# Attention and two gated layers: the score products of a head grouped by their number of rows

## The chip, the core and the metric

The kernel runs on one core of one Trainium2 chip. The metric is the device time of one execution in microseconds (us). TensorE (PE, with its weight loads listed apart as PEld), VectorE (DVE), ScalarE (ACT), GpSimd (POOL) and the DMA queues run beside each other and wait for each other by semaphores.

## The reference

The shapes are batch 2, 12 heads, 448 tokens, 64 dimensions a head; the model width is 768, the hidden width 1536. The operands of the three gated products arrive as float64 words, which the kernel decodes itself.

```python
scores = matmul(q, k^T) / sqrt(64)            # per batch and head: 448 x 448
scores = cap * tanh(scores / cap)
attn   = exp(scores - max) ; attn /= sum(attn)
x      = matmul(attn, v)                      # all heads side by side: 896 x 768
x      = (silu(x @ w_gate) * (x @ w_val)) @ w_out          # 768 -> 1536 -> 768
out    = (sigmoid(x @ w2_gate) * (x @ w2_val)) @ w2_out
```

## The kernel before

Precision is kept with float32r parts: a value is split into a high and a low part, and a product is the sum of high times high, low times high and high times low. In the attention, a head has only 64 dimensions, so the first two of the three terms are stacked into one product over 128 rows: the stationary operand `kk` holds k_high in 64 rows and k_low in the other 64, and the moving operand `qq` holds q_high twice. The third term, k_high times q_low (`kh`, `qlo`), has 64 rows.

The 24 heads are handled one after another, two to a pair. Within a head the keys are cut into four blocks of 112 (`CP`), and each block gives one 112 x 448 score tile in a PSUM bank of its own. `scores(n)` makes them in two halves. A half takes a two-bank tile `pss` from a pool of two such tiles (`bank2`), so the two halves of a head use the two buffers and the next head uses the same two again. For each of its two blocks, PE makes the 128-row product (line 410, which starts the sum) and then the 64-row product (line 411, which ends it). ACT then takes the tanh of the half (line 412) and, after both halves, the exponential of the whole head (line 416).

The order of work on every engine is written by hand in the loop over heads n. PE gets, in an even head: the 8 score products, 8 transposes for the pair after next (line 348), and the products of head n-2 with V (`values`, line 454). An odd head has the same without the transposes. In the values products a part of the blocks is computed in whole float32 and the rest in float32r parts (`eh`, `el`, `vh`, `vl`), all with 112 rows. Heads 0 to 3 are special: the first values products come ahead of head 2's scores, and there are none at all between heads 0 and 1 and between heads 2 and 3. DVE makes the parts and the normalisation (lines 352 to 356, 426, 428, 393, 397, 483, 468, 486), ACT copies each values result out (`xu`, line 457), POOL issues six small copies by DMA for each pair and makes `xl` (line 488). SP issues the loads and the DMAs of the denominators.

From head 21 on, DVE and ACT also decode the first weight blocks (lines 74 to 84). After the last head, PE alternates the first gated products (`products`, line 154) with the values of the last two heads; the last pair's `x` reaches them through line 488. Then follow the two gated layers.

Of the kernel before, what the change touches and what calls it, by code (L numbers as in the profile page):

```python
# [19 lines left out]
def attention_then_two_gated_layers(  # L20
# [14 lines left out]
    nc = tc.nc  # L35
    B, H, S, D = q.shape
# [3 lines left out]
    R = 4  # L40
    CP = S // R
# [4 lines left out]
    WIDEST = 32.0  # L46
# [5 lines left out]
    def bank2(name):  # L52
        return ps.tile([P, 2, 512], F32, tag="p2", name=name, bufs=2)
# [10 lines left out]
    wp = ctx.enter_context(tc.tile_pool(name="wp", bufs=2))  # L64

    def decode(r, hi, lo):
        """float64 words to hi + lo, each of which a float32r holds exactly or rounds last."""
        n = r.shape[1] * r.shape[2]
        w2 = r.rearrange("p k f -> p (k f)").bitcast(U32).rearrange("p (n two) -> p n two", two=2)
        low, top = w2[:, :, 0], w2[:, :, 1]  # L70
        t = wp.tile([P, n], U32, tag="t", name="t", bufs=1)
        c = wp.tile([P, n], U32, tag="c", name="c", bufs=2)
        g = wp.tile([P, n], F32, tag="g", name="g", bufs=1)
        nc.vector.tensor_scalar(t, top, 0x7FFFFFFF, 9, ALU.bitwise_and, ALU.logical_shift_right)  # L74
        nc.scalar.activation(c, t, AF.Relu, bias=bias_sb, scale=4096.0)  # L75
        yield
        nc.vector.tensor_scalar(g.bitcast(U32), top, 0x1FF, None, ALU.bitwise_and)
        nc.vector.scalar_tensor_tensor(g, low, 2.0**-32, g.bitcast(U32), ALU.mult, ALU.add)  # L78
        yield
        nc.vector.scalar_tensor_tensor(c, top, 0x80000000, c, ALU.bitwise_and, ALU.bitwise_or)  # L80
        nc.scalar.copy(hi, c.bitcast(F32).rearrange("p (k f) -> p k f", k=r.shape[1]))  # L81
        yield
        nc.vector.tensor_scalar(t, c, 0xFF800000, None, ALU.bitwise_and)
        nc.vector.scalar_tensor_tensor(  # L84
            lo,
            g.rearrange("p (k f) -> p k f", k=r.shape[1]),
            2.0**-20,
            t.bitcast(F32).rearrange("p (k f) -> p k f", k=r.shape[1]),
            ALU.mult,
            ALU.mult,  # L90
        )

    class Stream:
        """Weight blocks in the order of their use, loaded and decoded ahead of it."""

        def __init__(self, jobs):
            self.keys = list(jobs)
# [50 lines left out]
        return [bank1("pv0")[:, :S], bank1("pv1")[:, :S]]  # L148

    def products(o, w, bh, bl, u, ks, nk, off=0):  # L150
        """Adds the blocks ks of w^T x for half u of the tokens to o, in float32r parts."""
        for kk in ks:
            for m, (a, x) in enumerate(((w[0], bh), (w[0], bl), (w[1], bh))):
                nc.tensor.matmul(  # L154
                    o,
                    lhsT=a[:, kk - off, :],
                    rhs=x[:, kk, halves[u]],
                    start=(kk == 0 and m == 0),
                    stop=(kk == nk - 1 and m == 2),
                )  # L160

    # The weight blocks in the order they are decoded: 128 columns at a time, a layer's gate and
    # value in turn. The last product takes its weights as moving operand, in two wide blocks of
    # columns; the first of them is decoded during the second layer's gate and value.
    ZB = (320, 448)
    ZW = 64
    early = [(0, 4), (0, 9), (2, 2), (2, 4), (1, 5)]
# [34 lines left out]
            z_job(1, c)  # L202
        return Stream(jobs), pools, z_tiles

# [1 line left out]
    def hidden(ws, hp, sp, layer, func, bh, bl, begun):  # L206
        hh = hp.tile([P, KF, NT], F32R, tag="hh", name="hh")
        hl = hp.tile([P, KF, NT], F32R, tag="hl", name="hl")
# [76 lines left out]
                        m += rows  # L285
                e0 += ne

# [1 line left out]
    pairs = [(b, p) for b in range(B) for p in range(NP)]  # L289
    NPAIR = len(pairs)  # L290
    NHEAD = 2 * NPAIR
# [1 line left out]
    with ExitStack() as actx:  # L293
        ap = actx.enter_context(tc.tile_pool(name="ap", bufs=2))
        dr = actx.enter_context(tc.tile_pool(name="dr", bufs=2, space=bass.MemoryType.DRAM))
        fix = actx.enter_context(tc.tile_pool(name="fix", bufs=1))
        # Products of zeros that keep the tensor engine awake until the data comes.
        warm = ap.tile([P, 512], mybir.dt.bfloat16, tag="x", name="warm", bufs=2)
        nc.vector.memset(warm, 0.0)
        pw = bank1("pw")  # L300
# [38 lines left out]
            ]  # L339

        def transposed(i):
            """K and Q of a pair of heads with the head's dimension on partitions, as float32r
            parts, and stacked so that 128 rows carry k_hi q_hi + k_lo q_hi."""
            got = []
            for t in raw[i][:2]:
                pt = bank1("pt")
                for c in range(R):
                    nc.tensor.transpose(pt[:, c * CP : (c + 1) * CP], t[:, c, :, :], ident[:CP, :CP])
                got.append(pt[:, :S])
            pk, pq = got  # L350
            ka, kb, qa, qb, ql, kl = operand_tiles()
            nc.vector.tensor_copy(kb, pk)
            nc.vector.tensor_copy(qa, pq)
            yield
            nc.vector.tensor_tensor(kl, pk, kb.bitcast(F32), ALU.subtract)
            nc.vector.tensor_tensor(ql, pq, qa.bitcast(F32), ALU.subtract)
            nc.gpsimd.dma_start(qb[A], qa[Z])
            nc.gpsimd.dma_start(qb[Z], qa[Z])
            nc.gpsimd.dma_start(ka[A], kb[A])
            nc.gpsimd.dma_start(ka[Z], kl[A])  # L360
            nc.gpsimd.dma_start(kb[A], kl[Z])
            nc.gpsimd.dma_start(qa[Z], qa[A])
            operands[2 * i] = (ka, qa, ka[A], ql[A])
            operands[2 * i + 1] = (kb, qb, kb[Z], ql[Z])
            yield

        def transposed_apart(i, j, tiles, copy):
            """The same for one head of the pair, without the way over a DMA."""
            got = []
            for t in raw[i][:2]:  # L370
                pt = bank1("pt")
                for c in range(R):
                    nc.tensor.transpose(pt[A, c * CP : (c + 1) * CP], t[:, j, c, :], ident[:CP, :CP])
                got.append(pt[A, :S])
            pk, pq = got
            kk, qq, qlo = tiles[j], tiles[2 + j], tiles[4 + j]
            nc.vector.tensor_copy(kk[A], pk)
            copy(qq[A], pq)
            copy(qq[Z], pq)
            nc.vector.tensor_tensor(kk[Z], pk, kk[A].bitcast(F32), ALU.subtract)  # L380
            nc.vector.tensor_tensor(qlo[A], pq, qq[A].bitcast(F32), ALU.subtract)
            operands[2 * i + j] = (kk, qq, kk[A], qlo[A])
# [19 lines left out]
        def scores(n):  # L402
            kk, qq, kh, qlo = operands.pop(n)
            e = ap.tile([CP, R, S], F32, tag="e", name="e", bufs=3)
            for half in range(2):
                h = slice(2 * half, 2 * half + 2)
                pss = bank2("pss")
                for u in range(2):
                    c = slice((2 * half + u) * CP, (2 * half + u + 1) * CP)
                    nc.tensor.matmul(pss[:CP, u, :S], lhsT=kk[:, c], rhs=qq, start=True, stop=False)  # L410
                    nc.tensor.matmul(pss[:CP, u, :S], lhsT=kh[:, c], rhs=qlo, start=False, stop=True)  # L411
                nc.scalar.activation(e[:, h], pss[:CP, :, :S], AF.Tanh, scale=inv_sb[:CP])  # L412
                if n == 0:
                    nc.scalar.activation(e[:, h], e[:, h], AF.Exp, scale=near_sb[:CP])
            if n > 0:
                nc.scalar.activation(e, e, AF.Exp, scale=near_sb[:CP])
            ex[n] = e
# [17 lines left out]
        rb = {}  # L435

        def values(n):
            """The head's numerators and, in the row below them, denominators; both from whole
            float32 products or from float32r parts."""
            i, j = divmod(n, 2)  # L440
            e = ex.pop(n)
            tv = raw[i][2]
# [2 lines left out]
            if m:  # L445
                eh, el = eparts.pop(n)
                vh, vl = vparts.pop(n)
                for c in range(m):
                    w = R - m + c
# [42 lines left out]
            for _ in g:  # L492
                pass

        # How many of a head's key blocks go through float32r parts in the product with V, by what
        # the vector engine has time for beside the first weight blocks.
        nsplit = [0, 1, 2, 3] + [2, 3] * 9 + [1, 1]
        load(0, apart=True)
        cap_sb = const.tile([P, 1], F32, name="cap_sb")
# [84 lines left out]
    wide = nc.values_load(wide_sb[0:1, 0:1], min_val=0, max_val=1, skip_runtime_bounds_check_because="the result of a comparison")  # L584
    gated_layers(ws, pools, z_tiles, xh, xl, begun)

# [1 line left out]
    # Up to WIDEST the cap itself keeps exp(score) and the sums far inside of float32's range, and  # L588
    # the sums so far above the guard of 1e-9 (it is relative to the largest term) that it doesn't
    # reach their last place. Beyond, the attention is done over with the maximum of each row taken  # L590
    # off, and the guard.
    with tc.If(wide != 0):
        xh = const.tile([P, KD, NT], F32R, tag="xh", name="xh_any")
        xl = const.tile([P, KD, NT], F32R, tag="xl", name="xl_any")
        with ExitStack() as gctx:
# [9 lines left out]
            for b, p in pairs:  # L605
                kt = gp.tile([P, S], F32, tag="kt", name="kt")
                qt = gp.tile([P, S], F32, tag="qt", name="qt")
                for dst, src in ((kt, k), (qt, q)):
                    t = gp.tile([CP, R, 2, D], F32, tag="t", name="t")
# [5 lines left out]
                for j in range(2):  # L615
                    rows = slice(j * D, (j + 1) * D)
# [3 lines left out]
                    for c in range(R):  # L620
                        pss = bank1("pss")
# [67 lines left out]
```

## Time and profile before

| | |
|---|---|
| time of 3 runs | 690.79, 692.37, 692.53 us |
| median | 692.37 us |
| profiled execution, from its first to its last instruction (span) | 689.1 us |
| PE busy (matmul) | 681.2 us, 99% |
| DVE busy | 490.2 us, 71% |
| ACT busy | 297.1 us, 43% |
| granted TensorE clock, mean | 0.998 of full speed |

For the profiled execution the page gives its span and no time beside it; the median of the runs lies 3.2 us above the span, and the span is taken as the execution's time less these. A busy PE is not PE at its peak, since matmuls are pipelined and their ends are modelled: a row's own duration says little, and what a product costs is read from the distance between its start and the start of the next.

### The profile page before, as it was taken

The page shows a single profiled execution, that of the slowest core. Times are in us where ns is not written, and L with a number is a line of the kernel's source. Part 1 is how long each engine was busy: PE and PEld are TensorE (multiplying, and loading weights), DVE is VectorE, ACT ScalarE, POOL GpSimd, SP SyncE. Part 2 cuts the span into 40 slices and gives each one's busy share as a digit, 9 for nine tenths or more (in the row PEclk, how much of TensorE's full clock was granted, in tenths as well). Part 3 has the DMA queues.
Part 4 walks back from the last instruction along what each step waited for, and adds up shares of the span by engine and source line. Part 5 has one row for each costly group of instructions (what it writes and reads, how often), then busy time and mean ns, then how long its engine had stood idle before and what let it go on. Part 6 is the DMA issues. An engine that isn't in the chain of part 4 may idle for free. (4 is left out here: it accounts for less than half of the span.)

```text
span 689.1 us, 8475 instructions
## 1 busy us (share of the span) xinstructions
PE 681.2 (99%) x3218; PEld 567.0 (82%) x3218; DVE 490.2 (71%) x746; ACT 297.1 (43%) x369; POOL 46.5 (7%) x80
## 2 busy tenths in 40 slices
PE   9999999999999999999999999999999999999996
PEld 5455455458999999999999999999999999999995
DVE  6567877887798977799687976677798676495000
ACT  6767677762543443344343434333344333242000
POOL 1332333210000000000000000000000000000000
PEclk9999999999999999999999999999999999999999
DMA  8565756233224442344433443322344323062011
GB/s 204 104 133 127 191 135 153 53 106 119 93 93 137 138 137 93 92 137 138 136 113 119 142 133 119 111 92 92 103 143 142 117 92 92 26 205 67 27 41 31
DMA packets 107327, 77.98 MB, mean 113 GB/s; under 512 B 35472, under 2 KB 106512, under 8 KB 107280
## 3 DMA queue, kind: packets, MB, share of 16 engines
q1 hardware_dynamic: 102208, 70.28, 33.8%
q0 software_dynamic: 4800, 6.89, 4.7%
q8 instruction: 27, 0.44, 0.3%
q10 hardware_dynamic: 272, 0.20, 0.1%
q14 instruction: 20, 0.16, 0.1%
HBM read 67.63 MB, written 2.80 MB: 102 GB/s over the span
## 5 line engine op out<-in xcount | busy, mean ns | idle before, releaser
L75 ACT ACTIVATE c<-t,bias_sb 128x768 uint32<-128x768 uint32 x72 | 67.6, 940 | 88.4 <-DVE t L74 88.4
L81 ACT CAST wh<-c 128x768 fp32r<-128x768 f32 x60 | 50.3, 838 | 78.1 <-DVE c L80 78.1
L80 DVE SCALAR_TENSOR_TENSOR c<-r,c 128x768 uint32<-128x768 uint32 x72 | 68.5, 952 | 4.3 <-ACT c L75 4.2
L78 DVE SCALAR_TENSOR_TENSOR g<-r,g 128x768 f32<-128x768 uint32 x72 | 69.0, 958 | 2.5
L412 ACT ACTIVATE e<-pss,inv_sb 112x896 f32<-112x896 f32 x48 | 48.3, 1007 | 28.8 <-PE pss L411 22.1
L227 DVE TENSOR_TENSOR sg<-pv,sg 128x448 f32<-128x448 f32 x48 | 29.7, 619 | 43.1 <-PE pv L154 39.8
L84 DVE SCALAR_TENSOR_TENSOR wl<-g,t 128x768 fp32r<-128x768 f32 x60 | 58.3, 972 | 2.1
L228 ACT CAST hh<-sg 128x448 fp32r<-128x448 f32 x48 | 27.2, 567 | 72.3 <-DVE sg L227 71.6
L154 PE MATMUL pg<-xl,wh 128*128 128x448 f32 x144 | 52.8, 367 | 0.0
L154 PE MATMUL pg<-xh,wl 128*128 128x448 f32 x144 | 52.7, 366 | 0.0
L154 PE MATMUL pv<-yl,wh 128*128 128x448 f32 x144 | 52.7, 366 | 0.0
L154 PE MATMUL pv<-yh,wh 128*128 128x448 f32 x144 | 52.7, 366 | 0.0
L154 PE MATMUL pv<-xh,wh 128*128 128x448 f32 x144 | 52.7, 366 | 0.0
L154 PE MATMUL pg<-yh,wl 128*128 128x448 f32 x144 | 52.7, 366 | 0.0
L154 PE MATMUL pg<-yl,wh 128*128 128x448 f32 x144 | 52.7, 366 | 0.0
L154 PE MATMUL pg<-xh,wh 128*128 128x448 f32 x144 | 52.7, 366 | 0.0
L154 PE MATMUL pv<-xh,wl 128*128 128x448 f32 x144 | 52.7, 366 | 0.0
L154 PE MATMUL pg<-yh,wh 128*128 128x448 f32 x144 | 52.7, 366 | 0.0
L154 PE MATMUL pv<-xl,wh 128*128 128x448 f32 x144 | 52.7, 366 | 0.0
L154 PE MATMUL pv<-yh,wl 128*128 128x448 f32 x144 | 52.7, 366 | 0.0
L154 PE MATMUL pg<-hl,wh 128*128 128x448 f32 x144 | 52.6, 365 | 0.0
L154 PE MATMUL pg<-hh,wl 128*128 128x448 f32 x144 | 52.6, 365 | 0.0
(125 smaller groups left out, 1454.5 us busy)
## 6 DMA issues: line engine op xcount, KB each, us to landing
r<-in_moe_w_gate_dram SPq DMA_DIRECT2D x24, 768.0 KB, 4.3
r<-in_moe_w_val_dram SPq DMA_DIRECT2D x24, 768.0 KB, 4.3
r<-in_moe_w_out_dram SPq DMA_DIRECT2D x24, 768.0 KB, 4.2
vt<-in_v_dram SPq DMA_DIRECT2D x24, 112.0 KB, 3.2
rb<-d SPq DMA_DIRECT2D x12, 224.0 KB, 3.3
tk<-in_k_dram SPq DMA_DIRECT2D x10, 224.0 KB, 3.2
tq<-in_q_dram SPq DMA_DIRECT2D x10, 224.0 KB, 3.9
qb<-qa POOLq DMA_DIRECT2D x20, 112.0 KB, 2.3
```

Of the source, the lines that this page charges most:

```text
L75: nc.scalar.activation(c, t, AF.Relu, bias=bias_sb, scale=4096.0)
L78: nc.vector.scalar_tensor_tensor(g, low, 2.0**-32, g.bitcast(U32), ALU.mult, ALU.add)
L80: nc.vector.scalar_tensor_tensor(c, top, 0x80000000, c, ALU.bitwise_and, ALU.bitwise_or)
L81: nc.scalar.copy(hi, c.bitcast(F32).rearrange("p (k f) -> p k f", k=r.shape[1]))
L84: nc.vector.scalar_tensor_tensor(lo, g.rearrange("p (k f) -> p k f", k=r.shape[1]), 2.0**-20, t.bitcast(F32).rearrange("p (k f) -> p k f", ...
L154: nc.tensor.matmul(o, lhsT=a[:, kk - off, :], rhs=x[:, kk, halves[u]], start=(kk == 0 and m == 0), stop=(kk == nk - 1 and m == 2),)
L227: nc.vector.tensor_tensor(sg, vs[u], sg, ALU.mult)
L228: nc.scalar.copy(hh[:, f, halves[u]], sg)
L412: nc.scalar.activation(e[:, h], pss[:CP, :, :S], AF.Tanh, scale=inv_sb[:CP])
```

## The change

The four 128-row products of a head come first, then its four 64-row products. To do so both `pss` tiles are taken at the head's start. The products, their operands, the sum in each bank and the ACT instructions are the same as before. The rest of the diff empties docstrings and comments and leaves the code as it is.

```diff
         e = ap.tile([CP, R, S], F32, tag="e", name="e", bufs=3)
-            for half in range(2):
+            cols = [slice(c * CP, (c + 1) * CP) for c in range(R)]
+            banks = [bank2("pss") for _ in range(2)]
+            for c in range(R):
+                nc.tensor.matmul(banks[c // 2][:CP, c % 2, :S], lhsT=kk[:, cols[c]], rhs=qq, start=True, stop=False)
+            for c in range(R):
+                nc.tensor.matmul(banks[c // 2][:CP, c % 2, :S], lhsT=kh[:, cols[c]], rhs=qlo, start=False, stop=True)
+            for half, pss in enumerate(banks):
                 h = slice(2 * half, 2 * half + 2)
-                pss = bank2("pss")
-                for u in range(2):
-                    c = slice((2 * half + u) * CP, (2 * half + u + 1) * CP)
-                    nc.tensor.matmul(pss[:CP, u, :S], lhsT=kk[:, c], rhs=qq, start=True, stop=False)
-                    nc.tensor.matmul(pss[:CP, u, :S], lhsT=kh[:, c], rhs=qlo, start=False, stop=True)
                 nc.scalar.activation(e[:, h], pss[:CP, :, :S], AF.Tanh, scale=inv_sb[:CP])
```

## Rows read from the trace of the kernel before

**Rows 1.** The page: span, and busy time, share and instructions of the engines.
```profile
span 689.1 us, 8475 instructions
...
PE 681.2 (99%) x3218; PEld 567.0 (82%) x3218; DVE 490.2 (71%) x746; ACT 297.1 (43%) x369; POOL 46.5 (7%) x80
```

**Rows 2.** Busy time in stretches: engines in us (instructions), clock, DMA share, GB/s.
```profile
0.00:147.00 147.00, 145.52 (x531) 74.02 (x532) 110.56 (x199) 104.94 (x101) 45.10 (x79) 1.00 0.58 136
...
165.00:689.00 524.00, 517.75 (x2612) 479.84 (x2610) 365.61 (x525) 185.58 (x261) 0.00 (x0) 1.00 0.34 107
```

**Rows 3.** Timeline of PE, head 15: start us, duration us, line, out<-in, rows*columns.
```profile
95.03 0.57 PE L454 MATMUL pv<-el,vh 112*65 112x448 f32 x2
95.44 0.36 PE L410 MATMUL pss<-qb,kb 128*112 128x448 f32 x1
95.74 0.46 PE L411 MATMUL pss<-ql,kb 64*112 64x448 f32 x1
...
96.51 0.46 PE L411 MATMUL pss<-ql,kb 64*112 64x448 f32 x1
...
98.44 0.97 PE L454 MATMUL pv<-e,vt 112*65 112x448 f32 x2
...
101.07 0.37 PE L410 MATMUL pss<-qa,ka 128*112 128x448 f32 x1
```

**Rows 4.** Timeline of the weight loads of the same head, with idle time before.
```profile
95.24 0.18 PEld L410 LDWEIGHTS pss<-qb,kb 128*112 128x112 f32 x1
95.73 0.17 PEld L411 LDWEIGHTS pss<-ql,kb 64*112 64x112 f32 x1 [0.32 <-issue]
96.12 0.17 PEld L410 LDWEIGHTS pss<-qb,kb 128*112 128x112 f32 x1 [0.22 <-issue]
```

**Rows 5.** Waits of the weight loads, 0 to 165 us: us in total, times, longest.
```profile
PEld pss L411 <- issue: 22.2, 94, 0.3
```

**Rows 6.** Timeline of the engines, the lines of ACT for the scores of head 15.
```profile
97.00 1.01 ACT L412 ACTIVATE e<-pss,inv_sb 112x896 f32<-112x896 f32 x1 [0.83 <-DVE el L428]
...
98.55 1.01 ACT L412 ACTIVATE e<-pss,inv_sb 112x896 f32<-112x896 f32 x1 [0.54 <-PE pss L411]
...
99.59 1.79 ACT L416 ACTIVATE e<-e,near_sb 112x1792 f32<-112x1792 f32 x1
...
101.29 0.52 ACT L457 COPY xu<-pv 65x448 f32<-65x448 f32 x1
```

**Rows 7.** Timeline of PE, starts of heads 1, 2 and 3.
```profile
11.59 0.44 PE L410 MATMUL pss<-qb,kb 128*112 128x448 f32 x1
...
18.10 0.71 PE L410 MATMUL pss<-qa,ka 128*112 128x448 f32 x1
...
22.18 0.43 PE L410 MATMUL pss<-qb,kb 128*112 128x448 f32 x1
```

**Rows 8.** Timeline of ACT, the second tanh of heads 0 and 2.
```profile
10.62 0.99 ACT L412 ACTIVATE e<-pss,inv_sb 112x896 f32<-112x896 f32 x1
...
21.53 1.01 ACT L412 ACTIVATE e<-pss,inv_sb 112x896 f32<-112x896 f32 x1 [0.53 <-PE pss L411]
```

**Rows 9.** Busy time over one pair (heads 16 and 17), columns as in rows 2.
```profile
101.10:113.25 12.15, 12.15 (x47) 6.21 (x45) 9.59 (x17) 8.54 (x9) 4.61 (x7) 1.00 0.79 198
```

**Rows 10.** Timeline of DVE: first work of that pair, and of the next.
```profile
104.72 0.62 DVE L352 CAST kb<-pt 128x448 fp32r<-128x448 f32 x1 [2.52 <-PE pt L348]
...
116.86 0.62 DVE L352 CAST kb<-pt 128x448 fp32r<-128x448 f32 x1 [2.48 <-PE pt L348]
```

**Rows 11.** Busy time in heads 20 to 23, columns as in rows 2.
```profile
125.40:150.00 24.60, 24.60 (x80) 11.52 (x79) 20.36 (x37) 20.09 (x21) 2.54 (x2) 1.00 0.20 61
```

**Rows 12.** Timeline of DVE: the last pair's low part, and a decode step before it.
```profile
159.16 0.96 DVE L80 SCALAR_TENSOR_TENSOR c<-r,c 128x768 uint32<-128x768 uint32 x1 [1.76 <-ACT c L75]
...
170.03 0.63 DVE L488 TENSOR_TENSOR xl<-x,xh 128x448 fp32r<-128x448 f32 x1
```

**Rows 13.** Timeline of PE: the first product with that low part.
```profile
171.51 0.37 PE L154 MATMUL pg<-xl,wh 128*128 128x448 f32 x1
```

## The prediction

> **What bounds the kernel now.** Begin with the page's busy times: PE shows 99% of the span, far above DVE and ACT [rows 1]. A busy PE need not be a well-used one, so the next view is the busy time by stretch: in the attention (0 to 147 us) the weight loads are busy for half of the time, in the gated layers for 92% of it, and PE has next to no idle time in either [rows 2]. The same engine is thus full in both, but something in the attention makes its products longer. The timeline of PE shows what. Products of 112 rows follow each other at 0.205 us: two of them start at 95.03, the next group at 95.44 [rows 3]. The first score product after them has 128 rows and starts without a gap, so 112 and 128 rows go together. From there on 128-row and 64-row products alternate, and seven starts from 95.74 to 98.44 are (98.44 - 95.74) / 7 = 0.386 us apart, although each moves the same 448 columns. The weight loads tell why: the load for the first product is done 0.2 us ahead of it, during the product before, while from then on each load starts only when its own product is listed as starting, after 0.2 to 0.3 us of idle time [rows 4]. Of the 96 loads of 64-row weights, 94 waited so [rows 5]. So every change between 128 and 64 rows costs PE 0.386 - 0.205 = 0.18 us, about half on each side: the first score product, loaded ahead, is followed after 0.30 us (0.09 for the end of the old product), the others after 0.386 (0.09 more for the load in the open).
>
> That the two products of a block add into the same bank isn't the reason: the 112-row products of one head add into one bank too, at 0.205 us.
>
> **The change, part by part.** Removed are six of a head's eight changes of row count. Before: 128 to 64 four times, 64 to 128 or 112 four times (the last into what follows the head). After: one each. The operations are the same in number and shape. No DMA is issued in this step, so no queue is passed; ACT's order (tanh, tanh, exponential) stays.
>
> The saving is 6 x 0.18 = 1.08 us a head. The head in the rows takes 98.44 - 95.44 = 3.00 us for its score products and will take 1.92; 24 heads give 25.9 us, if two things hold.
>
> The first is that 64-row products follow each other as closely as 112- and 128-row products do. No row shows two of them in a row. The bounds are 0.205 us (the nearest rows by kind: float32r, 448 columns, one shape after the same shape) and 0.386 us (the nearest by operands: the same 64-row product among 128-row ones). I take 0.205, since the loads that come late in these rows all follow a product with another number of rows. At the upper bound the three steps from 64 to 64 save nothing and 24 x 3 x 0.18 = 13.0 us are lost; halfway (0.295, where only the load is in the open), 6.5.
>
> The rows show that a load hides behind a product of its own row count at 112 and 128 rows. The Trainium skill (TensorE: Matmul & The Clock Gate, Part 3, on what overlaps) says that a weight load overlaps with products in flight only when it goes to another row group. Taken at its word that would deny even the overlap that the 112-row loads have here, so the trace disagrees for full arrays; for 64 rows no run shows it. By the rule the 13.0 us would be lost, by the rows nothing.
>
> The second is that nobody else takes PE's place. Three engines or buffers come near.
>
> *Banks.* This is the wait that the change adds. The third product of a head now goes into the second tile, two products (0.41 us) after the head's start instead of 1.5 us after it. The tile must have been read by the tanh of the previous head's second half. Behind a PE that waits stand the rest of the head, the transposes and the values products; ACT's first tanh waits for it as well, because the product that ends the first half is now the sixth and no longer the fourth. The sixth starts 3 x 0.205 + 2 x 0.295 = 1.21 us after the head's start; the fourth did so after 96.51 - 95.44 = 1.07 [rows 3]. The tanh followed 97.00 - 96.51 = 0.49 us later [rows 6], so it now comes at +1.70. The second tanh will start right behind it, 1.04 later (99.59 - 98.55, one tanh with its gap), and end at about +3.75. The shortest heads in the middle are the odd ones, without transposes: 101.07 - 95.44 - 1.08 = 4.55 us [rows 3]; the third product of the next is at +4.96. So 1.2 us of cover remain, and no wait.
>
> In two places no values products lie between two heads. Head 1 starts at 11.59 [rows 7]; less head 0's 1.08 it would start at 10.51 and want the second tile some 0.45 later (two steps of 0.205, a little more behind transposes). Head 0's second tanh ends at 10.62 + 0.99 = 11.61 [rows 8] and doesn't come earlier, since its first tanh keeps its time: PE waits 0.6 us. Head 3 follows head 2 after 22.18 - 18.10 = 4.08 us, then 3.00, and wants its tile 0.45 later. Head 2's second tanh ended 21.53 + 1.01 - 18.10 = 4.44 after that head's start. It will end about 0.4 sooner: it comes 1.04 behind the first tanh instead of 98.55 - 97.00 = 1.55, and the first 0.14 later. That is 4.1 against 3.45. PE waits 0.6 us again. Loss: 1.2 us; nothing to 2 us are the bounds.
>
> *ACT.* Its instructions for a head are two tanh, the exponential and a copy [rows 6]: 1.04 + 1.04 + 1.70 + 0.52 = 4.3 us by their starts, 8.54 busy for a pair [rows 9], against a pair of 12.15 - 2.16 = 9.99. In the odd head it would end at 1.70 + 4.30 = 6.0, and the next tanh is wanted at 4.55 + 1.70 = 6.25. It fits.
>
> *DVE.* It is busy for 9.59 of a pair's 12.15 us [rows 9], without a break from 104.72 to 116.86 - 2.48 = 114.38, and then waits 2.5 us for the transposes of the next pair [rows 10]. That wait is the cover: it shrinks by 2.16 to some 0.3. DVE goes from 79% to 96% of the pair, and PE still ends last, by little. A late DVE wouldn't stop PE at once: `el` of a head is used a head later. The bounds: nothing lost, or, if DVE takes 0.5 us more per pair than now, 9 middle pairs x 0.2 = 1.8.
>
> At the end of the attention DVE and ACT decode weights besides. In heads 20 to 23 DVE is busy for 20.4 of 24.6 us [rows 11]; its 4.2 free us go to the 4 x 1.08 = 4.3 by which these heads get shorter, and it enters them about 1.1 later against PE than now (its last full list starts one head's gain earlier, the head after that two). It thus comes out some 1.2 us late (ACT, at 20.1 of the 24.6, likewise about 1 us, with what it makes used later still). Behind that it waits 1.76 us before the decode step at 159.16, which takes this up; and the low part of the last pair is ready at 170.03 + 0.63 = 170.66, while PE first uses it at 171.51 [rows 12, 13], so 0.85 us more could be late unseen. I take 0, with 0 to 2 as bounds.
>
> After that everything starts earlier by the same amount and is unchanged: the gated layers are PE's own 0.2 us steps [rows 2].
>
> Sum against the profiled execution: 689.1 - 25.9 + 1.2 = 664.4 us of span. The runs' median is 3.2 above the span, and I leave that difference as it is: 667.7 us, a gain of 24.7 us or 3.6%.
>
> **Rivals.**
> *A: 64-row products don't pipeline among themselves.* For it: no row shows the pair, and every 64-row load that the trace has came late. Against it: so did the 128-row loads between them, and these are quick elsewhere. Time: 667.7 + 13.0 = 680.7, or 674.2 at the half price.
> *B: DVE becomes the bound.* For it: 96% by the sum. Against it: its 9.59 us hold no wait, and the order of its work doesn't change. If a pair came out at 10.6 us instead of 9.99, 9 pairs would lose 5.5: 673.2.
> *C: the bank wait turns the gain around.* Then the third product of each head waits for the tanh of the head before. PE has 1.2 us of cover and gains 1.08, so it decides at a tanh 2.3 us later than worked out, in every head; at 2.7 us later the kernel would take 692.4 + 24 x 0.4 = 702. ACT's 8.54 us in a 9.99 us pair speak against it: the loop from a second tanh over the bank (0.2 for the rest of the 128-row products, 0.6 to the sixth, 0.5 to the tanh, 2.05 for two) is only 3.4 us long.
> *D: the change saves nothing,* because the cost hangs on each product and not on the change of rows. The 0.205 us between 112- and 128-row products speaks against it. Time: 692.
>
> **How the numbers follow.** Forecast 0.82 (664.5 to 671), A 0.09, B 0.06, C 0.01, D 0.02. A measurement of this kernel can't tell less than about 0.3% (2 us) from no change; the forecast, A and B lie beyond that: faster 0.97, same 0.02, slower 0.01. For 8 in 10 the range reaches from 664.5 (no wait at all in the first heads, or a slightly dearer change of rows) over B and A's half price to 675.5. A's full price is left out with C and D.
>
> **What would show it.** Right: the PE timeline of a head has four line 410 starts 0.2 us apart, then four of line 411, also 0.2 apart, and 1.9 us from the first to what follows; the late 64-row loads fall from 94 to about 24; DVE's wait for the transposes falls from 2.5 to some 0.3 us a pair; PE waits for ACT only in heads 1 and 3; a middle pair takes 10.0 us; the first gated product starts some 25 us earlier. Wrong: 0.386 or 0.295 between line 411 starts (A); a pair at DVE's length with PE waiting for `eh`, `el` or `vl` (B); PE waiting before the third product of middle heads (C). A gated stage of another length than now would be something that I have overlooked.

## The result, and the profile after

| | before | after |
|---|---|---|
| runs | 690.77, 690.79, 692.37, 692.53 us | 666.98, 667.83, 668.01, 668.05 us |
| median | 691.58 us | 667.92 us |
| span of the profiled execution | 689.1 us | 666.2 us |

The ratio of the times is 0.9652, with a 95% interval from 0.9629 to 0.9676. The forecast was 667.7 us.

The page after, in the lines that answer to [rows 1]:

```profile
span 666.2 us, 8475 instructions
...
PE 657.2 (99%) x3218; PEld 564.6 (85%) x3218; DVE 485.6 (73%) x746; ACT 294.4 (44%) x369; POOL 45.2 (7%) x80
```

The number of instructions is the same on every engine. The timeline of PE after, for two heads of one pair and the start of the next; equal neighbours are merged, with their number behind the x (line 408 is now the 128-row product, 410 the 64-row product, 455 the values product):

```profile
84.93 0.98 PE L408 MATMUL pss<-qa,ka 128*112 128x448 f32 x4
85.84 1.07 PE L410 MATMUL pss<-ql,ka 64*112 64x448 f32 x4
86.84 0.60 PE L348 MATMUL pt<-ident,tk 112*128 112x112 f32 x4
...
90.40 0.97 PE L408 MATMUL pss<-qb,kb 128*112 128x448 f32 x4
91.30 1.07 PE L410 MATMUL pss<-ql,kb 64*112 64x448 f32 x4
92.30 0.97 PE L455 MATMUL pv<-e,vt 112*65 112x448 f32 x2
...
94.92 0.98 PE L408 MATMUL pss<-qa,ka 128*112 128x448 f32 x4
```

The four 128-row products take 85.84 - 84.93 = 0.91 us, the four 64-row products 86.84 - 85.84 = 1.00 us. That is 3 x 0.205 + 0.295 and 0.09 + 4 x 0.205 + 0.09: the 64-row products follow each other as closely as the others. A head's scores take 1.91 us where they took 3.00 [rows 3], and the pair takes 94.92 - 84.93 = 9.99 us where it took 12.15 [rows 9]. The timeline of the weight loads, which answers to [rows 4]:

```profile
84.73 0.79 PEld L408 LDWEIGHTS pss<-qa,ka 128*112 128x112 f32 x4
85.84 0.68 PEld L410 LDWEIGHTS pss<-ql,ka 64*112 64x112 f32 x4 [0.32 <-issue]
86.84 0.39 PEld L348 LDWEIGHTS pt<-ident,tk 112*128 112x128 f32 x4 [0.32 <-issue]
```

Only the first load after a change of rows starts with its product; the first load of the 128-row group, which follows 112-row products, comes 0.2 us ahead of its own. Waits in the attention after, of the weight loads, of PE and of DVE (us in total, times, longest); the first answers to [rows 5]:

```profile
PEld pss L410 <- issue: 6.9, 22, 0.3
...
PE pss L408 <- ACT e L413: 0.8, 2, 0.6
...
DVE kb L352 <- PE pt L348: 14.8, 10, 3.2
```

Of the 64-row loads, 22 wait where 94 did. PE waits for ACT's tanh twice; the timeline of PE shows it in heads 1 and 3, as forecast, before their third product. The lines also show where the transposes or the values products behind these two heads' scores start:

```profile
10.13 0.64 PE L408 MATMUL pss<-qb,kb 128*112 128x448 f32 x2
11.34 0.65 PE L408 MATMUL pss<-qb,kb 128*112 128x448 f32 x2 [0.57 <-ACT e L413]
...
12.92 0.57 PE L373 MATMUL pt<-ident,trb 112*64 112x112 f32 x4
...
19.66 0.66 PE L408 MATMUL pss<-qb,kb 128*112 128x448 f32 x2
20.56 0.66 PE L408 MATMUL pss<-qb,kb 128*112 128x448 f32 x2 [0.24 <-ACT e L413]
...
22.14 2.47 PE L455 MATMUL pv<-e,vt 112*65 112x448 f32 x6
...
126.20 0.37 PE L154 MATMUL pg<-xh,wh 128*128 128x448 f32 x1
```

The last line is the first gated product. In the timeline of PE before it is this line:

```profile
150.99 0.37 PE L154 MATMUL pg<-xh,wh 128*128 128x448 f32 x1
```

So the attention alone gives 24.8 us. The span fell by 22.9 only: 1.9 us were given back later, 1.7 of it in one product that the change doesn't touch (below, the changed kernel once more).

### The profile page after: what moved, and what is told of

Read it like the earlier page. It is cut to its first block, busy times and chain, and to the rows that moved or that the text cites. A ratio compares the mean times of both kernels' runs of the same rounds, so it can differ in the third digit from the quotient of the medians.

```text
span 666.2 us, 8475 instructions
## 1 busy us (share of the span) xinstructions
PE 657.2 (99%) x3218; PEld 564.6 (85%) x3218; DVE 485.6 (73%) x746; ACT 294.4 (44%) x369; POOL 45.2 (7%) x80
## 5 line engine op out<-in xcount | busy, mean ns | idle before, releaser
L154 PE MATMUL pg<-hh,wh 128*128 128x448 f32 x144 | 53.0, 368 | 0.0
```

Of the source, the lines that this page charges most:

```text
L154: nc.tensor.matmul(o, lhsT=a[:, kk - off, :], rhs=x[:, kk, halves[u]], start=(kk == 0 and m == 0), stop=(kk == nk - 1 and m == 2),)
```

## The experiments

**The changed kernel once more.** No edit.

> The changed kernel once more, unchanged. Its gated stage, from the first gated product to the last product, took 533.2 us in the profile against 531.4 before, all of it in the first layer's output product, whose steps were 0.2067 us instead of 0.2027. Theory: this differs from one execution to the next of the same kernel, so another profile may show either step, and the times keep to 667 to 668 us. Rival: it belongs to the change (the stage starts earlier against the weight loads), and then every profile of this kernel shows 0.2067 there.

Measured: 667.99 us median (666.29 to 668.99). The profiled execution, at 668.99, again has the longer step. Busy time in 60 us of the first layer's output product, for before, after, and this run; the number behind PE's busy time is that of its products:

```profile
345.00:405.00 60.00, 60.00 (x297) 55.61 (x297) 48.82 (x69) 22.58 (x30) 0.00 (x0) 1.00 0.41 132
```
```profile
320.00:380.00 60.00, 60.00 (x292) 54.50 (x291) 48.20 (x68) 21.84 (x28) 0.00 (x0) 1.00 0.40 132
```
```profile
320.00:380.00 60.00, 60.00 (x292) 54.50 (x291) 48.21 (x68) 21.83 (x28) 0.00 (x0) 1.00 0.43 137
```

At the same granted clock, 297 or 292 products fit. From the starts in the timeline the step holds at 0.2027 or at 0.2067 us through that whole product (some 430 of them: 430 x 0.004 = 1.7 us), and is 0.204 in the other gated products of 448 columns. Both profiles of the changed kernel show the longer step, so the theory isn't shown directly. The runs below speak against the rival: equal rows, alternating, and the padded kernel with `xl` on VectorE alternate their products and have the longer step too, while the padded kernel reaches this product at nearly the same time as the changed one (306.9 us against 305.8) and has the shorter one. The times of a kernel also fall into groups about as far apart: of the 13 runs of before beside this one, eight lie from 690.5 to 691.1, three from 692.3 to 692.5, and two higher (694.3 and 696.9). What sets the step stays open.

**Grouped within each half.**

```diff
-            for c in range(R):
-                ... 128 rows into banks[c // 2]
-            for c in range(R):
-                ... 64 rows into banks[c // 2]
+            for two in (range(2), range(2, 4)):
+                for c in two:
+                    ... 128 rows into banks[c // 2]
+                for c in two:
+                    ... 64 rows into banks[c // 2]
```

> Grouped within each half only: two 128-row products, two 64-row, twice, so four changes of row count a head where there were eight before and two after. Theory (0.18 us for each change, nothing else): 24 x 4 x 0.18 = 17.3 us under before, about 674, and no wait for the banks in heads 1 and 3, so perhaps 1 us less. Rival (the gain comes from the long runs of four or from the order of the banks, and not from each change): well off 674, near 668 or near 691.

Measured: 674.14 us (673.94 to 674.37), ratio 0.9751 (0.9735 to 0.9768). The timeline of PE for head 15 of this kernel:

```profile
85.12 0.57 PE L409 MATMUL pss<-qb,kb 128*112 128x448 f32 x2
85.62 0.66 PE L411 MATMUL pss<-ql,kb 64*112 64x448 f32 x2
86.21 0.66 PE L409 MATMUL pss<-qb,kb 128*112 128x448 f32 x2
86.80 0.66 PE L411 MATMUL pss<-ql,kb 64*112 64x448 f32 x2
87.39 0.97 PE L456 MATMUL pv<-e,vt 112*65 112x448 f32 x2
```

The head's scores take 87.39 - 85.12 = 2.27 us, four changes less than 3.00: 4 x 0.18 = 0.72. The price is one for each change, whatever the length of the runs between.

**Both banks first, products alternating.**

```diff
             banks = [bank2("pss") for _ in range(2)]
-            for c in range(R):
-                ... 128 rows into banks[c // 2]
-            for c in range(R):
-                ... 64 rows into banks[c // 2]
+            for c in range(R):
+                ... 128 rows into banks[c // 2]
+                ... 64 rows into banks[c // 2]
```

> Both banks taken at the head's start as in the change, but the products alternate as before. Theory: no gain, 691 to 692, since the eight changes of row count stay. Rival (taking the banks early moves work or waits by itself): 1 us or more away from before, to either side.

Measured: 690.66 us beside 690.9 of before, ratio 0.9987 (0.9966 to 1.0009). Requesting both tiles at the head's start does nothing by itself. PE's order is that of before here, so the second tile's first product is still the head's fifth; what its earlier use costs shows only in heads 1 and 3 of the changed kernel.

**Equal rows, alternating.**

```diff
             for c in range(R):
                 ... lhsT=kk[:, cols[c]], rhs=qq, start=True, stop=False
-                ... lhsT=kh[:, cols[c]], rhs=qlo, start=False, stop=True
+                ... lhsT=kk[:, cols[c]], rhs=qq, start=False, stop=True
```

> Leaves out the low part of q: each 64-row product is replaced by a second copy of the block's 128-row product, in the alternating order of before. Theory (the cost hangs on the change of row count): steps of 0.205 us throughout, 24 x 8 x 0.18 = 34.6 us under before, about 657, or up to 4 us more where VectorE or ScalarE then hold a pair (9.27 us) up. Rival (the cost hangs on two products in turn into one bank, or on changing operands): about 691.

Measured: 664.33 us (661.87 to 666.91). The mechanism is confirmed and the time missed by 3 us at the upper end. In the timeline of PE all eight steps are at 0.2 us, two products in turn into one bank.:

```profile
84.78 0.37 PE L408 MATMUL pss<-qb,kb 128*112 128x448 f32 x1
84.98 0.36 PE L409 MATMUL pss<-qb,kb 128*112 128x448 f32 x1
85.18 0.36 PE L408 MATMUL pss<-qb,kb 128*112 128x448 f32 x1
...
86.39 0.92 PE L454 MATMUL pv<-e,vt 112*65 112x448 f32 x2
...
91.99 0.60 PE L348 MATMUL pt<-ident,tq 112*128 112x112 f32 x4 [0.76 <-DMA tq<-in_q_dram]
```

The scores take 86.39 - 84.78 = 1.61 us. Both products of a block have the same operands here, so this run says nothing on a change of operands; the padded kernel below does. But PE now waits for VectorE's parts and, in the last line, for a load of q. In the stretch from 80 to 104 us VectorE is busy for 23.8 of 24 us.

**96 rows against 128.**

```diff
             for c in range(R):
                 ... lhsT=kk[:, cols[c]], rhs=qq, start=True, stop=False
-                ... lhsT=kh[:, cols[c]], rhs=qlo, start=False, stop=True
+                ... lhsT=kk[:96, cols[c]], rhs=qq[:96], start=False, stop=True
```

> Leaves out the low part of q: as the run with equal rows in alternating order, but the second product of each block takes only the first 96 rows of the same operands. Theory (a change costs only where the rows fit in half of the array, 64 or fewer, since 112 and 128 go together): steps of 0.205 us, the time of the run with equal rows, about 657 to 661. Rival (any change in the number of 32-row groups costs): 0.386 us steps and about 691.

Measured: 661.37 us (two runs, 661.31 and 661.43). Timeline of PE:

```profile
84.86 0.37 PE L408 MATMUL pss<-qb,kb 128*112 128x448 f32 x1
85.06 0.37 PE L409 MATMUL pss<-qb,kb 96*112 96x448 f32 x1
85.28 0.37 PE L408 MATMUL pss<-qb,kb 128*112 128x448 f32 x1
...
86.52 0.92 PE L454 MATMUL pv<-e,vt 112*65 112x448 f32 x2
```

The scores take 1.66 us, 0.208 a step. 96 rows go with 128, as 112 do; 64 don't. The profiled execution is 2.6 us shorter than that of the run with equal rows; 1.7 of them are the step of the first layer's output product, 0.2067 us there and 0.2027 here. The Trainium skill (TensorEngine Tiling (Array Packing), Key Properties) says that a change of the array's tiling mode drains the engine, and under Available Configurations it lists tiles of 64 rows apart from those of 128. The runs agree that a change costs, and add the price: 0.18 us for each change here.

**No change of rows at all, the third term padded.** A head's low part of q goes into a 128-row tile of its own, zeros in the other head's rows; the third term takes the same weights `kk`. `scores` alternates by block, except in heads 1 and 3. Two other tiles get one buffer less to make room.

```diff
+        qz = [[fix.tile([P, S], F32R, name=f"qz{j}{m}") for j in range(2)] for m in range(3)]
+        for pair in qz:
+            for j, t in enumerate(pair):
+                nc.gpsimd.memset(t[(1 - j) * D : (2 - j) * D].bitcast(F32), 0.0)
...
-            nc.vector.tensor_tensor(ql, pq, qa.bitcast(F32), ALU.subtract)
+            nc.vector.tensor_tensor(z0[A], pq[A], qa[A].bitcast(F32), ALU.subtract)
+            nc.vector.tensor_tensor(z1[Z], pq[Z], qa[Z].bitcast(F32), ALU.subtract)
...
-            operands[2 * i] = (ka, qa, ka[A], ql[A])
-            operands[2 * i + 1] = (kb, qb, kb[Z], ql[Z])
+            operands[2 * i] = (ka, qa, ka, z0)
+            operands[2 * i + 1] = (kb, qb, kb, z1)
```

> Same result as the reference asks: the third term is made a 128-row product, with q's low part in the rows of its own head and zeros in the others, in the alternating order; heads 1 and 3 keep four 128-row and four 64-row products. VectorE writes the low part of q in two instructions of 64 rows (0.6 us more a pair). Theory: 22 heads lose the last two changes of row count, 22 x 2 x 0.18 = 7.9 us, so 660; up to 3 us more if VectorE (some 9.0 of 9.27 us a pair) holds PE up. Rival (a second pass over the same weights costs more than a change, or VectorE becomes the bound): 665 or more.

Measured: 667.37 us (665.46 to 668.62), no better than the change: the rival's figure, and of its two reasons the second. The steps are 0.205 us, although the moving operand changes with every product, and the first pairs take 9.33 us, but then four of the next five take 10.1 to 10.5. Waits of PE in the attention, and the timelines of VectorE, in a short pair and the long one behind it, and of GpSimd in the long one:

```profile
PE pv L462 <- DVE el L436: 2.6, 4, 0.7
PE pv L462 <- DVE vl L403: 1.6, 2, 0.8
```
```profile
88.63 0.85 DVE L434 CAST eh<-e 112x1344 fp32r<-112x1344 f32 x1
...
97.84 1.75 DVE L434 CAST eh<-e 112x1344 fp32r<-112x1344 f32 x1
```
```profile
97.70 1.17 POOL L496 TENSOR_TENSOR xl<-x,xh 128x448 fp32r<-128x448 f32 x1
```

VectorE has no free time left in the pair, and the same cast takes 0.85 us alone and 1.75 where GpSimd's `xl` runs.

**The same with `xl` on VectorE.**

```diff
-            (nc.gpsimd if i < NPAIR - 2 else nc.vector).tensor_tensor(xl[:, p, o], x, ...)
+            nc.vector.tensor_tensor(xl[:, p, o], x, ...)
```

> The padded kernel with the low part of x (xl) of every pair made by VectorE instead of GpSimd: 0.6 us more work a pair for VectorE. In the padded kernel PE waited for el, vl and vh, and VectorE's casts took 1.6 to 1.75 us instead of 0.4 to 0.85 wherever GpSimd's xl ran at the same time. Theory (VectorE binds, and it loses 1.2 us a pair to that overlap): a pair falls from 10.1 to about 9.6 us, the time to about 663 to 664. Rival (GpSimd's part doesn't disturb it, VectorE is merely full): a pair grows to 10.5 or more and the time to 671 or more.

Measured: 667.23 us (665.09 to 668.56), ratio 0.9645 (0.9625 to 0.9665): neither. The long casts are gone (0.85 us in the mean of ten), but the time is no shorter. Timeline of VectorE, first work of two pairs in a row and a wait between:

```profile
87.56 0.62 DVE L357 CAST kb<-pt 128x448 fp32r<-128x448 f32 x1
...
94.31 0.20 DVE L476 RECIPROCAL g<-g 112x8 f32<-112x8 f32 x1 [0.38 <-DMA g<-xu]
...
97.78 0.62 DVE L357 CAST kb<-pt 128x448 fp32r<-128x448 f32 x1
```

VectorE's own list is 97.78 - 87.56 - 0.38 = 9.84 us long, not the 9.6 assumed, and it waits for a DMA within it. In the padded kernel the same first work of successive pairs lies 9.21 us apart where `xl` meets none of VectorE's instructions, 10.2 to 10.6 us where it does, and 10.0 in the mean of six pairs. So the overlap did cost time, 0.8 us a pair and not the 1.2 assumed, but making `xl` costs VectorE nearly as much. What is left shows at the first gated product, which starts at 125.5 us instead of 126.6; this profile has the longer step of the output product, which takes 1.7 us back.

**And two key blocks instead of three in the odd heads.**

```diff
-        nsplit = [0, 1, 2, 3] + [2, 3] * 9 + [1, 1]
+        nsplit = [0, 1, 2, 2] + [2, 2] * 9 + [1, 1]
```

> As padded with xl on VectorE, and the odd heads take two instead of three key blocks through float32r parts in the product with V: some 0.75 us less a pair for VectorE, 0.16 us more for PE. Theory (VectorE binds at 9.6 us a pair, PE would need 9.27 + 0.16): PE binds again at 9.45 us, the time about 662. Rival (something else holds the pair): no gain on the run before it.

Measured: 663.08 us (662.39 to 665.36), ratio 0.9603 (0.9585 to 0.9621). In the timeline of PE the transposes of successive pairs are now 9.45 us apart in seven pairs in a row (the next takes 10.27, where VectorE waits 1.05 us for a DMA):

```profile
55.42 0.55 PE L352 MATMUL pt<-ident,tk 112*128 112x112 f32 x4
...
64.86 0.55 PE L352 MATMUL pt<-ident,tk 112*128 112x112 f32 x4
...
74.32 0.55 PE L352 MATMUL pt<-ident,tk 112*128 112x112 f32 x4
```

PE binds again, and the version is some 5 us faster than the change: its slowest run is below the fastest of the changed kernel's runs. The first gated product starts at 122.1 us where the change has 126.2, so 4.1 us come from the attention. The spans of the two profiles lie 5.7 us apart, and the other 1.6 are the step of the output product, which is the shorter one in this profile.

**The change with `xl` on VectorE.** The edit of the run before the last, made to the changed kernel.

> The changed kernel with xl of every pair on VectorE. Theory (PE binds there; VectorE has 1.5 us of waiting in each pair and no overlap with xl to lose): 0.6 us more work a pair changes nothing, 667 to 668. Rival (VectorE is already the bound of the changed kernel): 5 us more, or less, by what the overlap cost.

Measured: 667.75 us (665.7 to 667.9): no difference. In the changed kernel VectorE isn't the bound.

## Why the prediction was right, point by point

*The price of a change of rows* (0.18 us, 1.08 a head): right. The head fell from 3.00 to 1.91 us, the runs with four, eight and no changes lie where the price puts them by their scores, and neither the banks nor the operands have a part in it: products in turn into one bank step by 0.2 us (equal rows), and so do products whose moving operand changes each time (padded).

*64 rows after 64 rows at 0.205 us*: right; rival A is out. This was the largest open term, 13 us. By the rule that the prediction cites from the Trainium skill (TensorE: Matmul & The Clock Gate, Part 3, on what overlaps) they would lie further apart. The runs disagree: the four 64-row products of a head sit on the same rows, and they take 1.00 us with a change of rows at either end.

*The banks*: the place was right, two waits and both in heads 1 and 3. The idle times listed are 0.57 and 0.24 us instead of 0.6 and 0.6. By the starts the loss is larger: the scores of the two heads take 12.92 - 10.13 = 2.79 and 22.14 - 19.66 = 2.48 us, 0.9 and 0.6 more than the 1.91 of a middle head, so 1.45 us and not 1.2. The middle heads show no such wait; rival C is out.

*ACT*: it fits, as worked out.

*DVE*: the term was mis-sized, on the safe side. I put its wait for the transposes at 0.3 us in a middle pair; it is 1.55 to 1.57 us in four of six middle pairs, and 0.41 and 0.26 in the other two. Timeline of VectorE after, one pair of either kind, to compare with [rows 10], and busy time over a pair of the first kind, which answers to [rows 9]:

```profile
55.42 1.71 DVE L397 TENSOR_TENSOR vl<-vt,vh 112x130 fp32r<-112x130 f32 x2
57.54 0.62 DVE L352 CAST kb<-pt 128x448 fp32r<-128x448 f32 x1 [0.41 <-PE pt L348]
...
97.48 0.62 DVE L352 CAST kb<-pt 128x448 fp32r<-128x448 f32 x1 [1.57 <-PE pt L348]
```
```profile
84.90:94.90 10.00, 10.00 (x46) 6.09 (x46) 8.41 (x17) 8.35 (x9) 4.30 (x7) 1.00 1.02 235
```

The list is shorter, 8.41 us a pair busy instead of 9.59. In this row of the groups by line and shape, first before and then after, the cast of `vh` has become three times quicker (count, then us in total and ns of one):

```profile
L393 DVE CAST vh<-vt 112x130 fp32r<-112x130 f32 x10 | 10.7, 1067 | 0.0
```
```profile
L393 DVE CAST vh<-vt 112x130 fp32r<-112x130 f32 x10 | 3.1, 315 | 0.0
```

Before, GpSimd's `xl` ran beside that cast in every middle pair (head 17's: `xl` from 111.48, the two casts from 111.28 for 1.63 us; after, the two take 0.39, a difference of 1.24 us where the list lost 1.18). After, GpSimd's DMAs wait longer, and in four of six middle pairs `xl` falls into VectorE's free time; in the two others it runs beside the two `vl` of the pair, which take 1.71 and 1.85 us there instead of 0.56, and the wait is about what I forecast. The prediction had taken all of the 9.59 us for VectorE's own work. Rival B is out for the change; VectorE does bind in the kernels without any change of rows, where PE would need 9.3 us for a pair.

*The end of the attention*: no loss up to the first gated product, as taken. From head 0 to the first gated product the gain is 24.8 us against 24.7. Just behind it the cover of 0.85 us was used up, though: the first product with the last pair's low part starts 0.41 us after the product before it, where that step was 0.20 before, and in the profile of the changed kernel once more 0.66. The loss is a few tenths of a us, within the bounds of 0 to 2.

*The gated layers*: not quite unchanged. In the profile they are 1.8 us longer, by the step in one product. The span was forecast at 664.4 us and is 666.2. A second error lies against this one. The forecast adds 3.2 us from span to time, a median of three runs less the span of one execution; but the profiled execution after took 668.05 us, 1.85 more than its span, and in every run on record that lists both the two lie 1.7 to 1.9 us apart. The profile of before is thus one of an execution near 690.9 us, and the median of 692.37 belongs to the higher group. Too little span by 1.8 us and too much on top by 1.4 nearly cancel: that the median lies only 0.2 us from the forecast is luck. The medians lie 23.7 us apart. What the mechanism forecast is the gain in the attention, and that came out.

## What to carry to other kernels

Read PE by the distance between starts, by shape: where two shapes in alternation cost more than each in a row, the price hangs on the change, and sorting the products (independent sums, open in several banks) takes it away without touching the arithmetic. Here 64 rows must be kept apart from 112 and 128, while 96 go with 128, and filling 64 up with zeros costs PE no more than a plain 128-row product. After such a gain, work out each other engine's list for one period again, with undisturbed durations: here 7% less on PE (9.33 us a pair instead of 9.99) was enough to make VectorE the bound. And take span and time from the same execution.

## What the runs showed of the hardware that was not expected

A cast of VectorE from SBUF grew from 0.85 to 1.75 us, two casts in a row from 0.39 to 1.63, where a GpSimd tensor_tensor of 1.2 us ran at the same time. The Trainium skill (SBUF — State Buffer, Who interferes with whom) says that the two engines share a pair of ports, and that against a VectorE instruction in a mode with two ports whichever issues first holds the pair for its whole instruction while the other blocks. The rows agree in size: the cast that started at 97.84, beside an `xl` from 97.70 for 1.17 us, became 0.9 us longer, about what was left of `xl`. In which mode the casts ran no run shows. It means that a duration read from a trace can hold another engine's time, and changes when the schedule does.

One layer's output product, the same in every kernel, ran at a step of 0.2027 us in the profiles of some kernels and 0.2067 in those of others, at the same granted clock and constant from its first to its last product; all three profiles with the changed order have the longer one, but so have two of the alternating kernels. It is 1.7 us of 670. Why is open.
